# A quarter of the query weights as four loads of one row for each DMA engine, ahead of all other loads

## The chip, the core and the metric

The kernel runs on one core of a Trainium2 chip. The core has a matrix engine (PE), three engines for elementwise work (DVE, ACT, POOL), an engine that issues most transfers (SP), and 16 DMA engines that bring data from HBM into the on-chip memory of 128 partitions (SBUF). The time is the device time of one launch in microseconds (us), the median of several runs.

## The reference, cut to what matters

One token is decoded. It passes through attention over a cache of 65,536 positions (4 key/value heads, 32 query heads of 128) and, beside it, through a gated MLP; a sigmoid gate mixes the two results.

```python
q = (x @ wq).reshape(B, Sq, 32, 128)                    # x: 1 x 1024, wq: 1024 x 4096
scores = einsum('bhqd,bhkd->bhqk', q, k) * 128 ** -0.5  # k, v: 4 heads x 65536 x 128
a = einsum('bhqk,bhkd->bhqd', softmax(scores), v) @ wo  # wo: 4096 x 1024
z = gelu(x @ w_in)                                      # w_in: 1024 x 3584
b = (z[:1792] * (w_sp * layernorm(z[1792:]) + b_sp)) @ w_out
g = sigmoid((x * gate_w).sum())
out = g * a + (1 - g) * b
```

All of it is bf16. Everything that is read is 162 MB, of which the caches are 134 MB and the query weights `wq` 8.4 MB.

## The kernel before

**Loads.** All large loads stand in one list, `stream`, in a fixed order: the query weights, the first two pieces of K, W_in, two more pieces of K, W_out, and then K and V pieces in turn, and Wo in six loads at the end. Their target is a ring in SBUF, five slots of 16,384 bf16 elements a partition (32 KB): slots 0 to 2 mostly for K (`KR = 3`), from `VB = KR * SUB` on for V and the weights. `load` (L308) puts an entry into the list. `issue` (L377) issues entries in order, all on SP (L390), until one is reached whose place in the ring still holds something that hasn't been used; `done` (L399) marks a piece as used and calls `issue` again. What a load has to wait for is found by the recorder (`Recorder`, L18): every operation names what it reads and writes, and `plan` derives the semaphore waits. Each engine runs its own list in program order.

`rows(A_wq, 0, 8)` (L316) lays the 1024 rows of the query weights on 128 partitions, eight neighbouring rows each: partition p holds rows 8p to 8p+7, a run of 64 KB. The load is split over the 16 DMA engines, eight partitions each.

`emit` moves the first `R.ahead = 2` issues of SP (the query weights and the first K load) and the first four of ACT (x, the gate's weights and two scalars, L289) ahead of the barrier at the start of the program, so they are issued before the other engines begin.

**Around the query.** POOL and DVE first build constants (an identity `idb`, masks, selectors; L271 to L425). DVE spreads x over eight rows (`xm`, L428), PE turns it with eight small matmuls into the columns of `xT` (L433), so that column c holds x[8p + c] on partition p, and DVE copies it (L437). L438 to L452 bring the scalars and the gate into place. Then PE multiplies the eight columns with the query weights: for each column c four column groups times two halves, 64 matmuls of 512 columns into `ob`, four of which run side by side; it waits for `xT` and for the whole load of the weights:

```python
wqs, keys = use(("wq", 0))
def f(e):
    for c in range(KC):                      # KC = 8
        for cg in range(4):
            for s in range(2):
                ...                          # L261 / L263
P("PE", f, r=["xT"] + keys, w=["ob"])
done(("wq", 0))
```

After it the place of the weights is free and SP issues W_in. The query is copied, transposed and spread (L468 to L483) and POOL puts it into `qpad` (`q_piece`, L489), which is set to zero at the start (L275).

**The rest.** K pieces are transposed by DVE (L503) and multiplied with the query by PE (`k_piece`), followed by maximum, exponential (ACT, L535), transposition of the probabilities (L540) and the product with V (`pv_piece`). The MLP is done between the first K pieces. At the end PE multiplies with Wo (`wo_rows`, `wo_piece`, L713), the last quarter of which comes in three loads (`WO_CUT`), DVE copies the result (L776), and SP stores it (L367).

Of the kernel before, what the change touches and what calls it, by code (L numbers as in the profile page):

```python
# [138 lines left out]
def bass_gated_mix__gqa_block_cached__mixer_gmlp__decode_kernel(  # L139
# [22 lines left out]
    KC = D // 128  # L162
# [6 lines left out]
    SUB = 16384  # L169
# [15 lines left out]
    OFF = {}  # L185
    cur = 0

    def region(name, nbf):
        nonlocal cur
        OFF[name] = cur  # L190
        cur += (nbf + 15) // 16 * 16

    for name, n in [
        ("M16", 32), ("MQ", 32),
        ("RING", NSUB * SUB), ("KT", NKT * 4096), ("SC", NSC * 2048), ("PSB", 2 * 1024), ("PTSB", 2 * 1024),
        ("QPAD", 4 * QP), ("IDB", 128), ("BM", 256), ("SEL", 16 * 32),
        ("XT", KC), ("WB", 2), ("WBB", 4), ("ONEB", 128),
        ("MAXC", 2 * total), ("LP", 2 * total), ("COLS", 2 * 64), ("DM", 64), ("ONES", 256), ("QALL", 128), ("OVZ", 32 * OC + 31), ("E4Z", 128), ("MHALF", 4),
        ("YB", FC), ("OROW", QW),
    ]:  # L200
        region(name, n)
    NA = (cur + 63) // 64 * 64
    arena = nc.alloc_sbuf_tensor("arena", [128, NA], BF16)

    def ab(name, n, o=0):
        return arena[:, OFF[name] + o:OFF[name] + o + n]

    def af(name, n, o=0):
        return arena[:, OFF[name] + 2 * o:OFF[name] + 2 * (o + n)].bitcast(F32)

    def vw(base, off, dims, p0=0, np_=128):
        ps = base.ap[0][0]
        return bass.AP(tensor=base.tensor, offset=base.offset + off + p0 * ps,
                       ap=[[ps, np_]] + [list(d) for d in dims])

    idb, bm, ones = ab("IDB", 128), af("BM", 128), af("ONES", 128)
    sel, m16, mq = ab("SEL", 512), af("M16", 16), af("MQ", 16)
    xT, wb, wbb, oneb = ab("XT", KC), ab("WB", 2), af("WBB", 2), ab("ONEB", 128)
    qpad, qall = ab("QPAD", 4 * QP), ab("QALL", 128)
    maxc, lp, colt = af("MAXC", total), af("LP", total), af("COLS", 64)  # L220
    mhalf = af("MHALF", 2)
# [27 lines left out]
    ob, mb, fb = obt[:, :], mbt[:, :], fbt[:, :]  # L249
    tb = scp[:, 1024:1536]  # L250
    tbh = tb.bitcast(BF16)
    KSC = lambda n: ("scp", n % 2)
    KTB = ("scp", 1)

    R = Recorder()
    P = R.op

    def mm(e, loaded, *a, **kw):

        if not loaded:  # L260
            return e.matmul(*a, **kw)  # L261
        with nc.discard():
            one = e.matmul(*a, **kw).ins  # L263
        return e.add_instruction(dataclasses.replace(one, name=nc.get_next_instruction_name(), ldweights=False))
# [21 lines left out]
    def small(dst, src, key):  # L286
        def f(e):
            with nc.allow_non_contiguous_dma(reason="a few bytes"):
                return e.dma_start(dst, src)  # L289
        P("ACT", f, w=[key], dma="l" + key)  # L290
# [3 lines left out]
    xm = ab("SC", 1024, 3 * 2048 + 512)  # L294
# [8 lines left out]
    stream = []  # L303
    place = {}

    GRAN = 1024

    def load(keys, src, off):  # L308

        n = len(stream)  # L310
        w = src.shape[1]
        for i, key in enumerate(keys):
            place[key] = (n, off + i * (w // len(keys)), w // len(keys))
        stream.append((keys, off, src))

    def rows(w, i, c):  # L316

        return w[128 * c * i:128 * c * (i + 1), :].rearrange("(p c) n -> p (c n)", c=c)
# [9 lines left out]
    WQ_N = HQ * Dh  # L328
    VB = KR * SUB

    def load_k(n, slot):
        load([("k", n)], kv(A_k_cache, n), slot * SUB)

    def load_k2(n, slot):
        load([("k", n), ("k", n + 1)], kv(A_k_cache, n, True), slot * SUB)

    def load_v2(n, off):
        load([("v", n), ("v", n + 1)], kv(A_v_cache, n, True), off)

    load([("wq", 0)], rows(A_wq, 0, 8), VB)  # L340
    load_k2(0, 0)
    load([("win", 0)], rows(B_w_in, 0, 8), VB)
    load_k(2, 2)
# [2 lines left out]
    for i in range(6):  # L346
        a = 2 * i + 4
# [18 lines left out]
    def store():  # L366
        P("SP", lambda e: e.dma_start(out[0, 0].rearrange("(q n) -> q n", n=QW), osrc), r=["orow"],  # L367
          w=["out"], dma="out")

    issued = [0]  # L370
    used = set()
    owner = {}

    def grains(off, w):
        return list(range(off // GRAN, (off + w + GRAN - 1) // GRAN))

    def issue():  # L377

        while issued[0] < len(stream):
            n = issued[0]  # L380
            keys, off, src = stream[n]
            w = src.shape[1]
            gr = grains(off, w)
            if any(k not in used for x in gr if x in owner for k in owner[x]):
                return
            for j, x in enumerate(gr):
                owner[x] = (keys[j * len(keys) // len(gr)],)
            if n == len(stream) - 1:
                store()
            P("SP", lambda e, o=OFF["RING"] + off, w=w, src=src: e.dma_start(arena[:, o:o + w], src),  # L390
              w=[("slot", x) for x in gr], dma="s%d" % gr[0])
            issued[0] += 1

    def use(key):
        n, off, w = place[key]
        assert n < issued[0], key
        return arena[:, OFF["RING"] + off:OFF["RING"] + off + w], [("slot", x) for x in grains(off, w)]

    def done(key):  # L399
        used.add(key)  # L400
        issue()

    issue()


# [8 lines left out]
      r=["m32"], w=["sel"])  # L414
    P("DVE", lambda e: e.tensor_reduce(mq, vw(idf, 0, [[1, 16], [16, 8]]), AXX, ALU.add), r=["idf"], w=["mq"])
    P("DVE", lambda e: e.tensor_reduce(mhalf, vw(idf, 0, [[32, 2], [64, 2], [1, 32]]), mybir.AxisListType.XY, ALU.add),
      r=["idf"], w=["mhalf"])
# [3 lines left out]
    KSE = "sele"  # L421
    for fe in range(4):
        P("POOL", lambda e, fe=fe: e.tensor_copy(vw(sele, 128 * fe, [[32, 4], [1, 32]]),
                                                vw(idb, 64 * (fe // 2) + fe % 2, [[0, 4], [2, 32]])),
          r=["idb"], w=[KSE])  # L425


    P("DVE", lambda e: e.tensor_tensor(vw(xm, 0, [[128, 8], [1, 128]], 0, 8), vw(xrow, 0, [[0, 8], [1, 128]], 0, 8),  # L428
                                       vw(idb, 0, [[1, 8], [0, 128]], 0, 8), ALU.mult), r=[KX, "idb"], w=["xm"])

    def f(e):
        for c in range(KC):
            ins = e.matmul(tb[:, c:c + 1], vw(xm, c, [[8, 128]], 0, 8), oneb[0:8, 0:1], start=(c == 0),  # L433
                           stop=(c == KC - 1), skip_group_check=True)
        return ins
    P("PE", f, r=["xm", "oneb"], w=[KTB])
    P("DVE", lambda e: e.tensor_copy(xT, tb[:, 0:KC]), w=["xT", KTB])  # L437
    P("PE", lambda e: e.matmul(mb[:, 0:2], oneb[0:1, :], wb[0:1, :], start=True, stop=True),  # L438
      r=["oneb", "wsp", "bsp"], w=["mb"])
    P("DVE", lambda e: e.tensor_copy(wbb, mb[:, 0:2]), w=["wbb", "mb"])  # L440
# [5 lines left out]
      r=["ones", "gs"], w=[KTB])  # L446
# [4 lines left out]
      r=["g"], w=["omg"])  # L451
    P("DVE", lambda e: e.tensor_scalar(mhalf, mhalf, col(C_G), None, op0=ALU.mult), r=["mhalf", "g"], w=["mhalf"])  # L452


    wqs, keys = use(("wq", 0))

    def f(e):
        for c in range(KC):
            for cg in range(4):
                for s in range(2):  # L460
                    o = WQ_N * c + 512 * (4 * s + cg)
                    ins = mm(e, s > 0, ob[32 * cg:32 * cg + 1, 512 * s:512 * (s + 1)], xT[:, c:c + 1], wqs[:, o:o + 512],
                                   start=(c == 0), stop=(c == KC - 1), tile_position=(0, 32 * cg),
                                   skip_group_check=True)
        return ins
    P("PE", f, r=["xT"] + keys, w=["ob"])
    done(("wq", 0))
    P("DVE", lambda e: e.tensor_copy(psb[0:97, :], ob[0:97, :]), w=["psb", "ob"])  # L468
# [20 lines left out]
    def q_piece(g):  # L489
        for pb in range(4):  # L490
            P("POOL", lambda e, pb=pb: e.tensor_copy(vw(qpad, 24 + 32 * pb, [[QP, 4], [1, 8]], 32 * pb, 32),  # L491
                                                    vw(qall, 8 * g, [[32, 4], [1, 8]], 32 * pb, 32)),
              r=["qall"], w=["qpad"])

    nkt = [0]

    def k_piece(n, p):
        if n % NP == 0 and p == 0:
            q_piece(n // NP)
        sl, keys = use(("k", n))  # L500
        i = nkt[0]
        nkt[0] += 1
        P("DVE", lambda e: e.transpose(ktb(i).bitcast(F32), sl[:, 4096 * p:4096 * (p + 1)].bitcast(F32)),  # L503
          r=keys[4 * p:4 * p + 4], w=[("kt", i % NKT)])
        if p == 3:
            done(("k", n))

        def f(e):
            for fe in range(4):
                f2, ev = fe // 2, fe % 2  # L510
                o = QP * fe + 24 - 8 * p
                for b in range(2):
                    ins = mm(e, b > 0, sc_ps(n)[:, 512 * b:512 * (b + 1)], qpad[:, o:o + 128],
                                   vw(ktb(i), 2048 * b + 64 * f2 + ev, [[128, 16], [2, 32]]),
                                   start=(p == 0 and fe == 0), stop=(p == 3 and fe == 3), skip_group_check=True)
            return ins
        P("PE", f, r=["qpad", ("kt", i % NKT)], w=[KSC(n)])
# [258 lines left out]
    P("DVE", lambda e: e.tensor_copy(orow[0:W0 + NW, :], fb[0:W0 + NW, 0:QW]), w=["orow", "fb"])  # L776
    store()

    R.ahead = 2
    R.early = 4  # L780
    R.emit(nc)

# [27 lines left out]
```

## Time and profile before

| | us |
|---|---|
| median of 3 runs | 381.1 (380.82 to 381.35) |
| the profiled execution | 381.14 |
| its span, first to last instruction | 379.8 |
| DMA traffic in it | 162 MB, 427 GB/s over the span |
| PE busy | 231.7 |
| DVE busy | 204.5 |
| first load issued | 0.00 |
| query matmuls | 22.98 to about 29.5 |
| first K piece's transposes begin | 41.24 |
| last matmuls on Wo begin | 376.03 |
| output store issued | 378.59 |

Times in the profile are counted from the first instruction of the span. A line such as "L503" is a line of the kernel's file; L261 and L263 are the two lines of the helper `mm`, which records a matmul with and without a weight load. "SPq" is a transfer issued by SP. The DMA view of a short window cuts the window into 40 equal slices, and shows for each the busy share in tenths and the rate in GB/s; both are counted at the slice in which a packet starts if packets are longer than a slice. The records of single DMA packets (start, duration, size, queue) lie in the same trace: q1 is SP's queue, q10 ACT's, q8 and q14 bring instructions.

### The profile page before, as it was taken

What the parts mean: (1) busy time and instruction counts of PE and PEld (TensorE: products, weight loads), DVE (VectorE), ACT (ScalarE), POOL (GpSimd) and SP (SyncE); (2) the same over time, 40 slices, a digit from 0 to 9 for tenths busy, and PEclk for the clock granted to TensorE, in tenths of its full rate; (3) what the DMA queues carried; (4) which work ended last, traced back from release to release, by engine and by line L of the source; (5) the groups of instructions that cost most, each with busy time, mean ns of one, the idle gap of its engine ahead of it and who ended that gap; (6) DMA issues with size and microseconds to landing.
All of it is one profiled execution on the core that took longest, in us unless ns stands there. A gap on an engine that the chain in (4) does not pass through costs nothing.

```text
span 379.8 us, 2579 instructions
## 1 busy us (share of the span) xinstructions
PE 231.7 (61%) x1447; PEld 57.6 (15%) x836; DVE 204.5 (54%) x162; ACT 23.3 (6%) x24; POOL 9.4 (2%) x37
## 2 busy tenths in 40 slices
PE   0061389467558924894787129952895983639376
PEld 0010011011101200121111001220121110212024
DVE  4011496878379524965892248745874872312020
ACT  1000000010420000002100000022000000220010
POOL 6000000000000000000000000000000000000000
PEclk9997599698959975999799758985899896959789
DMA  9998999998999999999998999999999999989996
GB/s 435 435 428 386 469 388 438 435 470 377 437 442 442 435 437 435 435 400 442 478 435 386 428 442 442 443 442 428 428 397 437 473 442 442 430 386 424 431 430 271
DMA packets 4255, 162.17 MB, mean 427 GB/s; under 512 B 533, under 2 KB 533, under 8 KB 789
## 3 DMA queue, kind: packets, MB, share of 16 engines
q1 hardware_dynamic: 4208, 162.01, 99.0%
q8 instruction: 9, 0.15, 0.1%
q10 hardware_dynamic: 36, 0.00, 0.0%
q14 instruction: 2, 0.01, 0.0%
HBM read 162.01 MB, written 0.00 MB: 427 GB/s over the span
## 4 chain that ended last, share of the span: by engine, by line
DMA 64%; DVE 18%; PE 17%; issue 1%; ACTq 0%; SPq 0%; DVEq 0%
DMA arena<-in_A_k_cache_dram 41%; DVE arena L503 15%; DMA arena<-in_A_v_cache_dram 10%; DMA arena<-in_A_wo_dram 8%; DMA arena<-in_B_b_sp_dram 5%; PE scp L261 5%; PE scp L263 5%; PE obt L261 4%; PE obt L263 3%; DVE arena L540 1%; PE fbt L713 1%; ACTq L289 0%; DVE arena L574 0%; DVE arena L576 0%; SPq L390 0%
## 5 line engine op out<-in xcount | busy, mean ns | idle before, releaser
L503 DVE STREAM_TRANSPOSE arena<-arena 128x2048 f32<-128x2048 f32 x64 | 142.9, 2283 | 45.2 <-DMA arena<-in_A_k_cache_dram 31.1
L261 PE MATMUL scp<-arena 128*128 128x512 bf16 (+1 forms) x273 | 110.5, 421 | 85.4 <-DVE arena L503 84.9
L263 PE MATMUL scp<-arena 128*128 128x512 bf16 (+1 forms) x279 | 110.9, 416 | 0.3 <-issue 0.3
L261 PE MATMUL obt<-arena 128*64 128x512 bf16 (+2 forms) x334 | 62.7, 420 | 21.3 <-DMA arena<-in_A_v_cache_dram 21.3
L263 PE MATMUL obt<-arena 128*64 128x512 bf16 (+2 forms) x334 | 62.1, 416 | 0.0
L261 PEld LDWEIGHTS scp<-arena 128*128 128x128 bf16 (+1 forms) x275 | 27.4, 103 | 195.8 <-issue 97.7
L540 DVE STREAM_TRANSPOSE arena<-arena 128x2048 bf16<-128x2048 bf16 x7 | 16.2, 2311 | 29.5 <-PE obt L263 27.3
L261 PEld LDWEIGHTS obt<-arena 128*64 128x64 bf16 (+1 forms) x334 | 18.2, 113 | 74.4 <-issue 56.7
L535 ACT ACTIVATE arena<-arena 128x2048 bf16<-128x2048 f32 x8 | 16.0, 2002 | 218.1 <-DVE arena L532 195.0
L520 DVE TENSOR_SCALAR_CACHE_REDUCE arena<-scp 128x2048 f32<-128x2048 f32 x8 | 18.3, 2292 | 16.0 <-PE scp L263 16.0
L581 PE MATMUL mbt<-arena 128*128 128x128 bf16 x16 | 2.0, 267 | 12.6 <-DVE arena L576 12.6
L543 DVE STREAM_TRANSPOSE arena<-arena 128x1024 bf16<-128x1024 bf16 x2 | 2.5, 1247 | 12.5 <-PE obt L263 12.5
L491 POOL COPY arena<-arena 32x32 bf16<-32x32 bf16 x16 | 3.3, 204 | 233.5 <-PE scp L263 209.3
L569 DVE RECIPROCAL arena<-mbt 128x1 f32<-128x1 f32 x4 | 0.6, 139 | 15.8 <-PE mbt L564 15.8
L532 DVE TENSOR_REDUCE arena<-mbt 128x1 f32<-128x32 f32 x4 | 0.8, 192 | 14.0 <-PE mbt L529 14.0
L438 PE MATMUL mbt<-arena 1*128 1x2 bf16 x1 | 0.2, 158 | 12.6 <-DMA arena<-in_B_b_sp_dram 12.6
L440 DVE COPY arena<-mbt 128x2 f32<-128x2 f32 x1 | 0.2, 160 | 12.6 <-PE mbt L438 12.6
L433 PE MATMUL scp<-arena 8*128 8x1 bf16 x8 | 0.7, 199 | 8.3 <-DVE arena L428 8.3
L776 DVE CAST arena<-fbt 36x128 bf16<-36x128 f32 x1 | 0.3, 283 | 10.0 <-PE fbt L713 10.0
L713 PE MATMUL fbt<-arena 128*32 128x128 bf16 x128 | 4.1, 220 | 1.3 <-DMA arena<-in_A_wo_dram 1.3
L468 DVE CAST arena<-obt 97x1024 bf16<-97x1024 f32 x1 | 1.2, 1224 | 5.6 <-PE obt L263 5.6
L713 PEld LDWEIGHTS fbt<-arena 128*32 128x32 bf16 x128 | 3.6, 97 | 2.9 <-DMA arena<-in_A_wo_dram 1.9
(91 smaller groups left out, 54.9 us busy)
## 6 DMA issues: line engine op xcount, KB each, us to landing
arena<-in_A_k_cache_dram SPq DMA_DIRECT2D x6, 4096.0 KB, 33.1
arena<-in_A_v_cache_dram SPq DMA_DIRECT2D x2, 4096.0 KB, 26.8
arena<-in_B_w_in_dram SPq DMA_DIRECT2D x1, 7168.0 KB, 29.6
arena<-in_A_wo_dram SPq DMA_DIRECT2D x3, 2048.0 KB, 34.2
arena<-in_B_w_out_dram SPq DMA_DIRECT2D x1, 3584.0 KB, 20.6
arena<-in_A_wo_dram SPq DMA_DIRECT2D x1, 1280.0 KB, 30.9
arena<-in_A_wo_dram SPq DMA_DIRECT2D x1, 512.0 KB, 31.7
arena<-in_A_wo_dram SPq DMA_DIRECT2D x1, 256.0 KB, 31.4
```

Of the source, the lines that this page charges most:

```text
L261: return e.matmul(*a, **kw)
L263: one = e.matmul(*a, **kw).ins
L468: P("DVE", lambda e: e.tensor_copy(psb[0:97, :], ob[0:97, :]), w=["psb", "ob"])
L491: P("POOL", lambda e, pb=pb: e.tensor_copy(vw(qpad, 24 + 32 * pb, [[QP, 4], [1, 8]], 32 * pb, 32), vw(qall, 8 * g, [[32, 4], [1, 8]], 32 * ...
L503: P("DVE", lambda e: e.transpose(ktb(i).bitcast(F32), sl[:, 4096 * p:4096 * (p + 1)].bitcast(F32)), r=keys[4 * p:4 * p + 4], w=[("kt", i % ...
L520: P("DVE", lambda e: e.tensor_scalar(scs(j), scp[:, :], 0.0, None, op0=ALU.add, op1=ALU.max, accum_out=maxc[:, j:j + 1]), w=[("sc", j % 2) ...
L532: P("DVE", lambda e: e.tensor_reduce(gcol(g, K_NB), mb[:, 0:32], AXX, ALU.min), w=[("nb", g), "mb"])
L535: P("ACT", lambda e: e.activation(psb2, scs(j), ACTF.Exp, bias=gcol(j // 2, K_NB), scale=SCALE, accum_out=lp[:, j:j + 1]), r=[("sc", j % 2 ...
L540: P("DVE", lambda e: e.transpose(ptsb2, psb2), r=["psb"], w=[("ptsb", 0), ("ptsb", 1)])
L543: P("DVE", lambda e: e.transpose(ptsb(n), ab("PSB", 1024, 1024 * (n % 2))), r=["psb"], w=[("ptsb", n % 2)])
L581: ins = e.matmul(mb[:, 0:128], sel[:, 128 * c:128 * (c + 1)], osc[:, 128 * c:128 * (c + 1)], start=(c == 0), stop=(c == 3))
L713: ins = e.matmul(fb[32 * b:32 * (b + 1), 0:QW], ovz[:, z:z + 32], sl[:, o:o + QW], start=False, stop=(i == 3 and c == 7), tile_position=(0 ...
```

## The change

The query weights are split by rows. Rows 0 to 767 go as before, now six neighbouring rows (48 KB) on each of the 128 partitions. Rows 768 to 1023 come first, in four loads of 16 rows of the target: load r writes partitions 32 + r, 36 + r, ... 92 + r, each with four neighbouring rows (32 KB). They land in slot 2 of the ring, on partitions 32 to 95. The partitions 0 to 31 and 96 to 127 of that place are set to zero by DVE and POOL (`zp0`, `zp1`), so that the matmul can run over all partitions. `xT2` has ten columns more than `xT`, six for the large part and four for the small one; for the latter x runs past its end, into a stretch that POOL sets to zero (`xmz`), or meets the zeros of the weights. The matmuls run over ten columns of weights instead of eight and wait for all of the loads and for both memsets; W_in and the next K load wait for these matmuls. SP issues six loads ahead of the barrier instead of two.

```diff
-    xT, wb, wbb, oneb = ab("XT", KC), ab("WB", 2), af("WBB", 2), ab("ONEB", 128)
+    xT2, xT = ab("XT", 18), ab("XT", KC)
+    wb, wbb, oneb = ab("WB", 2), af("WBB", 2), ab("ONEB", 128)
...
+    NA4 = 4
+    KB6 = KC - 2
+    def load_a(r):
+        src = vw(A_wq, (128 * KB6 + NA4 * r) * WQ_N, [[1, NA4 * WQ_N]], 0, 1)
+        src = bass.AP(tensor=src.tensor, offset=src.offset, ap=[[4 * NA4 * WQ_N, 16], [1, NA4 * WQ_N]])
+        stream.append(((("wqa", 0),), 2 * SUB, src, r))
...
-    load([("wq", 0)], rows(A_wq, 0, 8), VB)
+    for r in range(4):
+        load_a(r)
+    load([("wq", 0)], rows(A_wq, 0, KB6), VB)
...
+            if r is not None:
+                for x in grains(off, w):
+                    owner[x] = keys
+                a = arena[:, OFF["RING"] + off:OFF["RING"] + off + w]
+                dst = bass.AP(tensor=a.tensor, offset=a.offset + (32 + r) * a.ap[0][0],
+                              ap=[[4 * a.ap[0][0], 16], [1, w]])
+                P("SP", lambda e, dst=dst, src=src: e.dma_start(dst, src), w=[("wqa", r)], dma="wqa%d" % r)
+                issued[0] += 1
+                continue
...
+    P("POOL", lambda e: e.memset(ab("SC", 128, 3 * 2048 + 512 + 1024), 0.0), w=["xmz"])
...
-        for c in range(KC):
-            ins = e.matmul(tb[:, c:c + 1], vw(xm, c, [[8, 128]], 0, 8), oneb[0:8, 0:1], start=(c == 0),
-                           stop=(c == KC - 1), skip_group_check=True)
+        at = [(c, 8) for c in range(KC)] + [(c, KB6) for c in range(KB6)] + [(128 * KB6 - 32 * NA4 + c, NA4) for c in range(NA4)]
+        for c, (o, st) in enumerate(at):
+            ins = e.matmul(tb[:, c:c + 1], vw(xm, o, [[st, 128]], 0, 8), oneb[0:8, 0:1], start=(c == 0),
+                           stop=(c == len(at) - 1), skip_group_check=True)
         return ins
-    P("PE", f, r=["xm", "oneb"], w=[KTB])
-    P("DVE", lambda e: e.tensor_copy(xT, tb[:, 0:KC]), w=["xT", KTB])
+    P("PE", f, r=["xm", "xmz", "oneb"], w=[KTB])
+    P("DVE", lambda e: e.tensor_copy(xT2, tb[:, 0:KC + KB6 + NA4]), w=["xT", KTB])
+    zp = [af("RING", SUB // 2, SUB)[32 * i:32 * (i + 1), :] for i in (0, 3)]
+    P("DVE", lambda e: e.memset(zp[0], 0.0), w=["zp0"])
+    P("POOL", lambda e: e.memset(zp[1], 0.0), r=[KSE, "xmz"], w=["zp1"])
...
+    wqa = ab("RING", NA4 * WQ_N, 2 * SUB)
+    keys = keys + [("wqa", r) for r in range(4)] + ["zp0", "zp1"] + [("slot", x) for x in grains(2 * SUB, SUB)]
+    used.add(("wqa", 0))
...
-        for c in range(KC):
+        parts = [(wqa, c) for c in range(NA4)] + [(wqs, c) for c in range(KB6)]
+        for i, (w, c) in enumerate(parts):
+            z = KC + (KB6 + c if w is wqa else c)
...
-              r=["qall"], w=["qpad"])
+              r=["qall", "zp1"], w=["qpad"])
...
-    R.ahead = 2
+    R.ahead = 6
```

More of the change, by code (lines that the diff above doesn't have):

```diff
@@ L196, in bass_gated_mix__gqa_block_cached__mixer_gmlp__decode_kernel @@
         ("QPAD", 4 * QP), ("IDB", 128), ("BM", 256), ("SEL", 16 * 32),
-        ("XT", KC), ("WB", 2), ("WBB", 4), ("ONEB", 128),
+        ("XT", 18), ("WB", 2), ("WBB", 4), ("ONEB", 128),
         ("MAXC", 2 * total), ("LP", 2 * total), ("COLS", 2 * 64), ("DM", 64), ("ONES", 256), ("QALL", 128), ("OVZ", 32 * OC + 31), ("E4Z", 128), ("MHALF", 4),
@@ L313, in load @@
             place[key] = (n, off + i * (w // len(keys)), w // len(keys))
-        stream.append((keys, off, src))
+        stream.append((keys, off, src, None))
     def rows(w, i, c):
@@ L380, in issue @@
             n = issued[0]
-            keys, off, src = stream[n]
+            keys, off, src, r = stream[n]
             w = src.shape[1]
+            if r is not None:
[7 more added lines that the diff above has]
+                continue
             gr = grains(off, w)
@@ L461, in f @@
                     o = WQ_N * c + 512 * (4 * s + cg)
-                    ins = mm(e, s > 0, ob[32 * cg:32 * cg + 1, 512 * s:512 * (s + 1)], xT[:, c:c + 1], wqs[:, o:o + 512],
-                                   start=(c == 0), stop=(c == KC - 1), tile_position=(0, 32 * cg),
+                    ins = mm(e, s > 0, ob[32 * cg:32 * cg + 1, 512 * s:512 * (s + 1)], xT2[:, z:z + 1], w[:, o:o + 512],
+                                   start=(i == 0), stop=(i == len(parts) - 1), tile_position=(0, 32 * cg),
                                    skip_group_check=True)
```

## The prediction

> **What bounds the kernel now.** I read the page first, for which engine carries the span, then the chain of waits, then the DMA view in short windows at both ends of the run, then the timeline around the query projection.
>
> ```profile
> q1 hardware_dynamic: 4208, 162.01, 99.0%
> q8 instruction: 9, 0.15, 0.1%
> ...
> DMA 64%; DVE 18%; PE 17%; issue 1%; ACTq 0%; SPq 0%; DVEq 0%
> ```
>
> The first line says that the packets of SP's queue fill 99.0% of what 16 DMA engines could do in 379.8 us. Sixteen 64 KB packets of 2.418 us each (the median of the packet records) make 434 GB/s, and every packet's median added up and divided by 16 is 374.2 us. The last line is the chain of waits: mostly landings, with DVE and PE work behind them. No DMA engine idles between 2 and 375 us. So the time is: when the engines begin, plus 374.2 us, plus what delays an engine, plus the tail behind the last landing. The changed loads are the very first ones, so I looked at 0 to 3 us, in 40 slices of 0.075 us, where GB/s counts a packet in the slice in which it starts (one 64 KB packet is 874):
>
> ```profile
> DMA  0000000000000999900900009090000000000000
> GB/s 0 0 1 0 0 0 0 0 0 0 0 0 0 5243 1748 1748 1748 0 0 1748 0 0 0 0 874 0 874 0 0 0 0 0 0 0 0 0 0 0 0 0
> ```
>
> SP issues the first load at 0.00. Six engines start at 1.00 us, six more by 1.27, then two at 1.45, one at 1.81, one at 1.96: a stagger of 0.96. By the records the first packets end at 4.07 to 4.67. Less the normal 2.418, the engines have in effect begun at 1.65 to 2.25, so most first packets hold about 0.65 us of extra (3.07 against 2.42; the last starter only 0.05). The lag isn't worked off; 18 to 24 us, in slices of 0.15 us:
>
> ```profile
> GB/s 0 0 0 437 3932 1311 437 874 0 0 0 0 0 0 0 0 0 0 0 0 3495 2185 437 874 0 0 0 0 0 0 0 0 0 0 0 0 3495 2185 437 874
> ```
>
> Three rounds of packets, each 2.42 us after the last, each with a pack and three stragglers. The middle round, at 21.0, is the first of the K load: the boundary between two loads costs nothing visible. The other end, 375 to 378 us (0.075 us a slice), and the output store, 378.5 to 379.5 (0.025 us):
>
> ```profile
> DMA  9975969899984819284837455544242900000000
> ```
>
> ```profile
> GB/s 0 0 0 0 0 0 0 0 0 0 0 0 0 0 0 0 0 0 0 0 0 0 0 0 0 0 0 0 0 0 0 0 0 0 20 31 21 10 0 0
> ```
>
> From 376 on only about nine engines still work, until 377.43. The page counts nine instruction packets (q8, 16 KB each); the records put eight of them before the end, each 0.88 to 0.97 us long and with one data packet of about 0.5 us extra behind it. So a hit costs one engine some 1.4 us, and the hit engines are those that end last; among them the ends are about 0.45 us apart. The last line is the store of one small packet for each of eight engines: issued at 378.59, its packets start at 379.37 to 379.44, that is 0.78 us after the issue and within 0.07 us. What follows the last landing:
>
> ```profile
> 376.03 2.16 PE fbt L713 x64
> 378.28 0.28 DVE arena L776
> ```
>
> Wo's last three pieces feed those 64 matmuls, which had waited for DMA at 373.05 (1.07 us) and 376.03 (0.26); an earlier landing passes on to the end one for one, up to about 1 us.
>
> **The change part by part.** *The first load.* It removes one load of 128 rows of 64 KB (eight packets an engine) and puts in four of 16 rows of 32 KB (one packet an engine) and one of 128 rows of 48 KB. Bytes stay. Start of the first packets: the nearest row for one packet an engine is the store, 0.78 us and a stagger of 0.07, against 1.00 and 0.96 now; an upper end is that nothing moves. I take the store's row, since its shape is that of the new load. Of the 0.65 extra I keep all (bounds: 0.05, as the last starter shows, and 0.76, the longest). In effect the engines then begin at 0.78 + 0.65 = 1.43 to 1.50. The engine that began first gains 0.22 us, the last one 0.75. Which of them ends last isn't in the records; the 0.45 us spread among the late enders looks like the start's, so I count a gain of 0.22 + 0.33 = 0.55.
>
> *Its price.* Four more load boundaries: the one at 21.0 us lies within the 2.42 rhythm to some 0.02 us, so 4 x 0.02 = 0.08. Four 32 KB packets take 4 x 1.213 = 4.85 and eight of 48 KB some 14.52 (from 28 KB: 1.062 and 56 KB: 2.116), together 0.03 over eight of 2.418. Sum 0.1 us. From above: no boundary in this trace has its next load issued only 0.4 us before it, so one could cost the first packet's 0.65 each time; that is the slow rival.
>
> [...]
>
> *The query projection.* It grows from 16 groups of four matmuls (0.43 us each until 28.9 us) to 20: +1.7 us at most; ten more transposing matmuls are +0.8 (eight took 0.66). Two new memsets of 8192 f32 a partition: L282's 1024 in 0.91 us makes 7.3 us on DVE, L277's 1055 in 0.98 makes 7.6 on POOL, from about 10 us on; DVE's delays L440 to about 18 us, POOL's the wait of q_piece. Side by side both end by 18, one after the other by 25; the weights land at 22. Small POOL memset: 0.2 us ahead of the x transposes. What covers this:
>
> ```profile
> 22.98 0.60 PE L261 MATMUL obt<-arena 128*1 128x512 bf16 x4
> 29.56 0.33 SPq L390 DMA_DIRECT2D arena<-in_B_w_in_dram  x1
> 32.38 0.94 POOL L491 COPY arena<-arena 32x32 bf16<-32x32 bf16 x4 [23.71 <-DVE arena L483]
> 41.24 4.50 DVE L503 STREAM_TRANSPOSE arena<-arena 128x2048 f32<-128x2048 f32 x2 [8.92 <-DMA arena<-in_A_k_cache_dram]
> ```
>
> The query has to be there by 41.24 and SP's W_in issue by 40.35, when its first packet follows K's. In the worst order the projection ends at 25 + 6.5 + 1.7 = 33.2 and the query stands at 37: nothing on the path, 7 us left for the issue. Queued behind SP's wait (now also for the matmuls on the new rows) are W_in and the next K load, both behind the same wait already. The b_sp chain (L438, 21.53) comes earlier, as its eight turns behind 64 KB packets become four behind 32 and four behind 48 KB.
>
> *SP's six issues ahead.* 0.37 to 0.42 us each, 2.3 us in all against 0.85. The other engines start at 2.25, half a microsecond after ACT's last issue; now perhaps 2.8. All of that set-up waits for weights at 22 us.
>
> *PE's code.* About 44 more PE instructions on 2283 (some 254 for each instruction packet) move the hits some 7 us forward and add none before the end. A second hit on one engine would cost 1.4.
>
> Sum: 381.14 for the profiled execution (379.83 and 1.31 around it; the median is 0.04 lower), -0.55 + 0.10 = -0.45, so 380.65 from the median; I say 380.6.
>
> **The rivals.** *Fuller gain:* the late enders are late starters (0.75), and the smaller first packets hold less extra (0.65 down to 0.3): 1.1 - 0.1 = 1.0, 380.1. For it: the last starter's packet had hardly any extra. Against: the fifteen others had 0.44 to 0.76. *Nothing:* what comes before 1.65 us is the memory's waking, not the load's shape, and the engines that end last began early: 0.1 less at most, 381.0. For it: packets started from 1.00 to 1.27 all end at 4.07 to 4.29. *Bubbles (slower):* with one packet an engine, each load runs dry before the next one's packet is there, and the 0.65 is paid four more times: 381.1 - 0.55 + 2.6 = 383.2. It decides once a following load's packets arrive over 1.21 us after the previous ones. Against: SP's issues are 0.43 apart. *Late query:* W_in's issue passes 40.35; it takes 11 us of new delay where I find 4 at most. With a second instruction hit (382.0) it shares a small chance.
>
> **How the numbers follow.** Forecast 0.37, fuller gain 0.36, nothing 0.14, bubbles 0.09, late query or second hit 0.04. About 0.2%, 0.76 us, is what a measurement of this kernel can tell from no change: under 380.34 is faster, over 381.86 slower. The forecast's own spread (0.2 to 0.85 gained) puts 0.08 of its 0.37 below 380.34. Faster: 0.36 + 0.08 = 0.44; same: 0.29 + 0.14 = 0.43; slower: 0.09 + 0.04 = 0.13. The range goes from the fuller gain with its extra all gone (381.1 - 0.78 - 0.60 + 0.1 = 379.8) to 381.5, "nothing" with boundaries at 0.1 each; bubbles stay outside.
>
> **What would show it.** Right: in the first 3 us sixteen packets start within 0.2 us of each other, before 1.0; later rounds show no stragglers; the last data packet ends near 376.9; W_in is issued between 28 and 34 us. Wrong: slices without packets between 1.5 and 7 us (bubbles), first starts still at 1.0 with stragglers (nothing), DMA idle near 40 us (late query), or a last engine with two q8 packets.

## The result: slower, 382.33 us against 380.92

The changed kernel takes 382.33 us (382.13 to 382.55), the one before 380.92 in the same comparison: a ratio of 1.0036, with a 95% interval of 1.0026 to 1.0046, or 1.41 us more. The profiled execution of the changed kernel has a span of 380.9 us.

The page of the changed kernel: the traffic is the same, the share of the queue lower, and the chain of waits again mostly landings.

```profile
q1 hardware_dynamic: 4336, 162.01, 98.7%
q8 instruction: 9, 0.15, 0.1%
...
DMA 57%; DVE 20%; PE 20%; ACT 1%; SPq 1%; issue 1%; DVEq 0%
```

The DMA view from 0 to 3 us in slices of 0.075 us (a 32 KB packet is 437, the small figures are ACT's tiny loads), and SP's timeline, with the first line of the one before for comparison:

```profile
DMA  0000000000000000009999900900909000000000
GB/s 0 0 0 0 0 0 0 0 0 0 0 0 0 0 17 10 0 0 1748 874 1748 874 437 0 0 437 0 0 437 0 437 0 0 0 0 0 0 0 0 0
```

```profile
0.00 2.51 SPq L401 DMA_DIRECT2D arena<-in_A_wq_dram  x4
2.55 0.59 SPq L411 DMA_DIRECT2D arena<-in_A_wq_dram  x1
3.19 0.44 SPq L411 DMA_DIRECT2D arena<-in_A_k_cache_dram  x1
```

Before:

```profile
0.00 0.37 SPq L390 DMA_DIRECT2D arena<-in_A_wq_dram  x1
```

The first packet starts at 1.36 us, not earlier than before (1.00) but later, and the last engine starts at 2.26: the stagger is still 0.90. Each small load holds SP for 0.57 to 0.64 us, and the 48 KB load behind them for 0.59, where the one large load took 0.37. From 0 to 8 us, in slices of 0.2 us (a 32 KB packet is 164, a 48 KB packet 246):

```profile
DMA  0000009995330007993004995900999993339999
GB/s 0 0 0 0 0 10 655 1147 328 164 164 164 0 0 0 330 1481 657 164 0 0 164 819 983 164 492 0 0 328 328 492 328 655 164 164 164 737 1229 983 492
```

The second round starts around 3.2 us, the third around 4.5. The fourth should follow 1.21 us later, around 5.7, and be as narrow as the second; it is smeared from 5.7 to 7.0. By the packet records, the packets of the third round last up to 2.31 us instead of 1.21, those of the engines that escaped there are lengthened in the fourth, and some of the first 48 KB packets by 0.1 to 0.3. After 8 us the rounds are regular again, but an engine's delay stays with it; 18 to 24 us, 0.15 us a slice, the rounds now in two clusters:

```profile
GB/s 0 0 983 983 1638 983 328 328 0 0 0 0 0 0 655 1311 1311 1311 328 328 0 0 0 0 0 0 0 2185 2185 1748 437 437 0 0 0 0 0 0 0 0
```

At the other end, 376 to 379 us (0.075 us a slice), the last data packet ends at 378.41, 0.98 later than before, and one engine works alone for its last 0.2 us. What follows is as long as it was:

```profile
DMA  7969695946374656462545443219000000000000
```

```profile
377.04 2.16 PE fbt L744 x64
...
379.29 0.28 DVE arena L807
```

To put one number on the start, take for each engine the time less the normal durations of the packets that it has moved so far (the last one in part), and the mean over the 16 engines: the **lag**. At 20 us it is 1.84 us before the change and 2.94 after it, 1.10 more. It consists of the mean start of the first packets (1.24 and 1.61), the mean lengthening of packets (0.60, all in the first ones, and 1.16) and, after the change, 0.1 to 0.2 of idle gaps. As the end waits for the latest engine, a second number helps: the last of the sixteen first packets of W_in starts at 40.93 before and 42.11 after, 1.18 later. These come from one execution of each kernel, the times are medians; the two profiled executions themselves took 381.14 and 382.29, 1.15 apart.

### The profile page after: what moved, and what is told of

It is laid out like the page before. It is cut to its first block, busy times and chain, and to the rows that moved or that the text cites. A ratio compares the mean times of both kernels' runs of the same rounds, so it can differ in the third digit from the quotient of the medians.

```text
span 380.9 us, 2632 instructions
## 1 busy us (share of the span) xinstructions
PE 235.4 (62%) x1473; PEld 58.6 (15%) x854; DVE 211.1 (55%) x163; ACT 23.3 (6%) x24; POOL 16.4 (4%) x39
## 4 chain that ended last, share of the span: by engine, by line
DMA 57%; DVE 20%; PE 20%; ACT 1%; SPq 1%; issue 1%; DVEq 0%
DMA arena<-in_A_k_cache_dram 34%; DVE arena L534 17%; DMA arena<-in_A_v_cache_dram 9%; DMA arena<-in_A_wo_dram 8%; PE scp L262 6%; PE scp L264 5%; DMA arena<-in_A_wq_dram 5%; PE obt L262 4%; PE obt L264 4%; DVE arena L571 2%; SPq L401 1%; PE fbt L744 1%; ACT arena L566 1%; PE fbt L692 0%; ACT arena L688 0%
## 5 line engine op out<-in xcount | busy, mean ns | idle before, releaser
L262 PE MATMUL obt<-arena 128*64 128x512 bf16 (+2 forms) x342 | 64.3, 420 | 21.8 <-DMA arena<-in_A_v_cache_dram 20.3
L264 PE MATMUL obt<-arena 128*64 128x512 bf16 (+2 forms) x342 | 63.6, 415 | 0.0
L462 DVE MEMSET arena<- 32x8192 f32 x1 | 6.9, 6885 | 1.6 <-issue 1.6
L463 POOL MEMSET arena<- 32x8192 f32 x1 | 6.9, 6920 | 0.1
```

Source lines behind the costliest of these rows:

```text
L462: P("DVE", lambda e: e.memset(zp[0], 0.0), w=["zp0"])
L463: P("POOL", lambda e: e.memset(zp[1], 0.0), r=[KSE, "xmz"], w=["zp1"])
```

## The experiments

All times are medians, all differences are against the kernel before in the same comparison. "Small" is a load of fewer than 128 rows. Start, lengthening, lag and W_in are each read from one execution, so small differences in them say little; where start and lengthening do not add up to the lag, the rest is idle gaps.

| kernel, loads in order | mean start | lengthening | lag at 20 us | latest W_in | time | difference | 95% interval of the ratio |
|---|---|---|---|---|---|---|---|
| before: 128 x 64 KB | 1.24 | 0.60 | 1.84 | 40.93 | 380.92 | | |
| changed: 4 of 16 x 32, 128 x 48 | 1.61 | 1.16 | 2.94 | 42.11 | 382.33 | +1.41 | 1.0026 to 1.0046 |
| e1: 64 x 32, 128 x 48 | 1.64 | 0.50 | 2.13 | 41.04 | 381.33 | +0.41 | 0.9999 to 1.0016 |
| e9: 2 of 64 x 16, 128 x 48 | 1.57 | 0.60 | 2.16 | 41.23 | 381.36 | +0.35 | 1.0000 to 1.0018 |
| e10: 4 of 64 x 8, 128 x 48 | 1.53 | 1.00 | 2.60 | 42.05 | 382.14 | +1.13 | 1.0020 to 1.0043 |
| e6: 8 of 16 x 16, 128 x 48 | 1.57 | 1.78 | 4.00 | 43.35 | 383.19 | +2.25 | 1.0045 to 1.0069 |
| e2: 128 x 48, 4 of 16 x 32 | 1.35 | 0.83 | 2.20 | 42.01 | 381.57 | +0.65 | 1.0010 to 1.0028 |
| e17: 128 x 48, 64 x 32 | 1.17 | 0.96 | 2.13 | 41.79 | 381.53 | +0.62 | 1.0009 to 1.0026 |
| e18: 128 x 48, 128 x 16 | 1.26 | 0.80 | 2.05 | 41.45 | 381.61 | +0.56 | 1.0005 to 1.0023 |
| e7: 2 of 128 x 32 | 1.22 | 0.62 | 1.82 | 41.00 | 381.02 | +0.08 | 0.9993 to 1.0010 |
| e14: 4 of 128 x 16 | 1.22 | 0.77 | 2.08 | 41.22 | 381.23 | +0.21 | 0.9997 to 1.0014 |
| e15: 8 of 128 x 8 | 1.62 | 0.22 | 1.80 | 41.03 | 381.06 | +0.04 | 0.9992 to 1.0010 |
| e16: before, with the new work beside | 1.22 | 0.66 | 1.88 | 40.79 | 380.93 | +0.02 | 0.9992 to 1.0010 |

**e1, one small load.** The same rows in the same places, as one load.

```diff
-    for r in range(4):
-        load_a(r)
+    load_a(0)                       # ap=[[NA4 * WQ_N, 64], [1, NA4 * WQ_N]] onto partitions 32 to 95
...
-    R.ahead = 6
+    R.ahead = 3
```

> One load of 64 rows on the partitions 32 to 95 takes the place of the four loads of 16; rows, places, memsets and matmuls stay as in the changed kernel. Theory 1 (the loss comes from four small loads issued one after the other into empty queues): first packets at 1.0 to 1.3 us, no lengthened packets after the first ones, 381.0 to 381.3. Theory 2 (the loss comes from the new memsets and matmuls): 382.3. Theory 3 (rows on half of the partitions, or rows of 48 KB, are slow to load): 382 or more, with long packets in every round of the first load.

381.33, just above theory 1's range and far below the other two. No packet after the first round is lengthened by more than 0.07 us, so places and rows are not slow. But the first packet is still late, at 1.41, and SP's issue took 0.60. Its first 3 us:

```profile
GB/s 0 0 0 0 0 0 0 0 0 0 0 0 0 0 24 3 0 0 437 2621 874 874 0 437 437 0 0 0 1311 0 0 0 0 0 0 0 0 0 0 0
```

**e2, the large load first.**

```diff
+    load([("wq", 0)], rows(A_wq, 0, KB6), VB)
     for r in range(4):
         load_a(r)
-    load([("wq", 0)], rows(A_wq, 0, KB6), VB)
```

> The load of 48 KB rows is issued first, then the four loads of 16 rows, then K; all else as in the changed kernel. Theory 1 (small loads cost only while the queues are empty): first packets at 1.0 as before the change, the four small loads at 4 x 1.21 us without extra, 381.0 to 381.2. Theory 2 (memsets, matmuls): 382.3. Theory 3 (the small loads are slow in themselves): their packets are over 1.3 us long here too, 381.8 or more.

381.57. The first packet is at 1.01 and SP's first issue takes 0.37, and the small loads' own packets, now at 16 to 22 us, are not lengthened: theory 3 falls. The time fits none of the three: 0.65 us are lost, in first packets of 48 KB that last up to 1.8 us longer than normal. That was not expected; e17, e13 and e18 take it up.

**e3 and e4, what else happens at that time.** e3 issues only the four small loads ahead of the barrier, e4 takes ACT's tiny loads out.

```diff
e3:  R.ahead = 6  ->  R.ahead = 4
e4:  R.early = 4  ->  R.early = 0
```

> Only the four small loads are issued ahead of the barrier, the 48 KB load and K behind it. Packets lengthened by 0.3 to 1.1 us stand between 4.4 and 7.5 us in the changed kernel. If the descriptors of the two large loads cause them, they come about 1.5 us later here, and the time stays at 382.3. If the other engines' start behind the barrier (4.0 us in the changed kernel) causes them, they come about 0.8 us earlier. If the large loads' packets arrive too late, slices without packets appear near 6 to 7 us, and it is 383 or more.

> ACT issues its four tiny loads behind the barrier, no longer beside SP's first issues. If ACT's issues are what lengthens SP's from 0.37 to 0.58 to 0.64 us and moves the first packet from 1.00 to 1.36, these go back to 0.4 and 1.0, and the time is 381.7 to 382.0. If it is the form of the loads (every fourth partition), they stay, and so does 382.3.

e3: 382.19 (+1.27, 1.0022 to 1.0046). e4: 382.34 (+1.42, 1.0023 to 1.0048). Neither moves the loss. In e3 the large loads were issued only 0.6 and 0.4 us later (3.16 and 3.55), not 1.5 as I had thought, and the long packets again start mostly in the third and fourth rounds, between 4.3 and 6.1 us (one stands at 3.4); so e3 rules out the other engines' start as the cause, which came 0.88 earlier (3.15 instead of 4.03), but not the large loads. In e4 SP's issues still take 0.57 to 0.59 and the first packet stays at 1.40: ACT's loads are not it.

**e5, two loads of 32 rows on every second partition.**

```diff
-            ap=[[4 * NA4 * WQ_N, 16], ...]      # source;  target every fourth partition
+            ap=[[2 * NA4 * WQ_N, 32], ...]      # source;  target every second partition, r = 0, 1
```

> Two loads of 32 rows (two 32 KB packets an engine) take the place of the four of 16. Lag is the time less what the bytes moved so far take at normal packet durations, the mean over the 16 engines at 20 us: 1.84 us before the change, 2.94 with four loads, 2.13 with one. Theory 1a (each small load more costs its share while the queues are empty): lag about 2.4, time 381.7. Theory 1b (only from the third load on are packets lengthened, as seen): lag about 2.1 to 2.2, 381.3 to 381.4. If loads of half of the partitions start late whatever their number, the first packets stay at 1.36 to 1.45.

385.38 (+4.44, 1.0102 to 1.0173), and no answer to its question: after the first ones the packets of the two loads lasted about 2.37 us instead of 1.21, which alone is 4.6 us for four packets an engine. The profiled execution is not a typical one: it took 390.33, the other five 385.34 to 385.43. Which engine writes which row of such a load isn't in the records.

**e6, eight small loads.**

```diff
-    for r in range(4): load_a(r)       # 16 rows of 32 KB
+    for r in range(8): load_a(r)       # 16 rows of 16 KB: half r % 2 of the rows of load r // 2
...
-    R.ahead = 6
+    R.ahead = 10
```

> Eight loads of 16 rows of 16 KB (0.61 us a packet) take the place of the four of 32 KB; SP issues ten loads ahead of the barrier. If SP's rate of issue (0.58 to 0.64 us for such a load) is what the engines wait for, they now stand still or have lengthened packets between nearly all loads: lag 4.0 to 5.5, time 383.4 to 385. If the cost is one of bytes or of places (partitions 32 to 95), lag and time stay near 2.9 and 382.3.

383.19, lag 4.00, of which 0.65 is idle gaps between packets: bytes and places are the same in sum, so small loads in front are paid by their number, or by how little each holds (256 KB here, 512 KB in the changed kernel). Its first 8 us show the smearing of all rounds from the second on:

```profile
GB/s 0 0 0 0 0 10 246 737 82 246 85 85 988 82 82 328 328 410 82 246 164 164 246 328 492 328 246 328 246 246 574 246 164 492 246 164 328 410 164 410
```

**e7, e14, e15: two, four and eight loads of 128 rows,** with no other part of the change but eight more transposing matmuls.

```diff
-    load([("wq", 0)], rows(A_wq, 0, 8), VB)
+    for i in range(n):                          # n = 2, 4, 8
+        load([("wq", i)], rows(A_wq, i, 8 // n), VB + 8 // n * i * WQ_N)
...
-    R.ahead = 2
+    R.ahead = n + 1
```

> The kernel before, with the query weights as two loads of 128 rows of 32 KB (four rows each) instead of one of 64 KB; no memsets, no matmuls more. If the late first packet (1.36 to 1.41 instead of 1.00) belongs to loads on fewer than 128 partitions, it is at 1.00 here, the lag 1.85 to 1.95 and the time 380.9 to 381.1. If it belongs to rows of 32 KB or to any split of the first load, it is at 1.3 to 1.4, with 381.2 to 381.5.

> The kernel before with the query weights as four loads of 128 rows of 16 KB, issued one after the other ahead of the barrier. If any three or more loads issued in the first microseconds lengthen packets: lag 2.3 to 2.9, 381.5 to 382.3. If only loads of fewer than 128 rows do: lag 1.85, 381.0, as with two loads of 128 rows.

> The same with eight loads of 128 rows of 8 KB, nine issues ahead of the barrier. By count: lag near 4 (as with eight loads of 16 rows), 383. By form: lag 1.9 to 2.0 (64 packets of 8 KB an engine, a few ns more each), 381.0 to 381.3.

381.02, 381.23 and 381.06; two and eight are the kernel before within 0.1 us; four lose 0.21 with an interval that reaches down to no difference, and a lag of 2.08 between the two that were expected. The lag with eight is 1.80, against 4.00 with eight small ones. So it is not the number of loads alone, nor rows shorter than 64 KB, nor issues in quick succession. First packets are at 0.99 to 1.05 in all three. For the late start this separates rows from bytes: e1 and e14 begin with 2 MB, e9 and e15 with 1 MB, and those of 64 rows are late, those of 128 are not. For the lengthened packets it does not: the kernels that pay for several loads in front (the changed one, e6, e10) have 256 or 512 KB in each load, and the kernels that do not pay (e7, e9, e14, e15) have 1 MB or more. Loads of 128 rows with 512 KB in each were not tried.

**e8, the kernel before without ACT's loads in front.**

```diff
-    R.early = 4
+    R.early = 0
```

> The kernel before with ACT's four tiny loads behind the barrier. If these, issued beside SP's first, are what spreads the first packets over 0.96 us, all sixteen start within 0.3 us, the lag falls to about 1.6 and the time to 380.6 or 380.7, under both kernels. If not, the lag stays at 1.8 to 1.9 and the time at 380.9.

381.00 (0.9992 to 1.0010), lag 1.90. The stagger isn't ACT's either.

**e9, e10: two and four loads of 64 rows.**

```diff
-    for r in range(4): load_a(r)       # 16 rows of 32 KB
+    for r in range(n): load_a(r)       # n = 2: 64 rows of 16 KB;  n = 4: 64 rows of 8 KB
```

> Two loads of 64 rows of 16 KB on the partitions 32 to 95 take the place of the four of 16 rows of 32 KB. (The earlier two loads on every second partition were at half the rate, 2.36 us for 32 KB, so they could not tell what a second load costs.) Lag was 2.13 us with one load, 2.94 with four, 4.00 with eight, some 0.27 for each more. If the number of loads into empty queues is what costs: lag 2.4, time 381.5 to 381.7. If only loads with one row for each engine cost: lag 2.1 to 2.2, 381.3.

> Four loads of 64 rows of 8 KB on the partitions 32 to 95. If the number of loads counts: lag 2.9, lengthened packets between 4 and 8 us, time 382.2 to 382.4, as with four loads of 16 rows. If the form with one row for each engine counts: lag 2.1 to 2.3, 381.3 to 381.5.

Two: 381.36, no more than one, so my 0.27 for each load was wrong between one and two. Four: 382.14, with packets lengthened from 4.6 us on and in ten of the sixteen first 48 KB packets. So one row for each engine is not the point; four loads of 64 rows cost nearly what four of 16 cost (both are 512 KB a load, and 1 MB in the run with two). The window from 4 to 8 us with two loads (slices of 0.1 us), for comparison with the smeared one above, has its rounds of 0.6 us and then the 48 KB packets close together:

```profile
GB/s 492 164 328 330 499 661 661 164 164 492 328 819 655 164 0 655 328 819 655 164 0 655 328 655 655 164 164 983 983 1966 1475 983 492 983 492 0 0 0 0 0
```

**e11, the large load third.** Two small loads, the 48 KB load, the other two.

```diff
-    for r in range(4):
+    for r in range(2):
         load_a(r)
     load([("wq", 0)], rows(A_wq, 0, KB6), VB)
+    for r in range(2, 4):
+        load_a(r)
```

> The changed kernel with the 48 KB load issued third, after two small loads and before the other two. If small loads cost only until a large load has filled the queues: lag 2.3 to 2.5 and no lengthened packets where the last two small loads run, time 381.4 to 381.7. If the third load's packets are lengthened whatever it is, or the small loads cost in any place: lag 2.8 or more, 382.1 or more.

382.24 (+1.23, 1.0020 to 1.0045), lag 2.53, latest W_in 42.14. Lag said the one and time the other; I go by the time. The packets lengthened are now, but for one, 48 KB packets that start between 4.9 and 6.8 us, two by 0.7 and 0.8, the rest by 0.1 to 0.3: the time in the run is nearly the same, the load that is hit another. So it isn't only the small loads' own packets that are slow.

**e12, 64 rows from partition 0 on** (a single execution).

> One look at the first packets only: one load of 64 rows of 32 KB as in the run with one load, but on the partitions 0 to 63. If a load is late because it has fewer than 128 rows, SP's issue takes 0.57 to 0.60 us and the first packet starts at 1.36 to 1.45. If it is late because it does not begin at partition 0, they are 0.37 and 1.00. [...]

SP's issue takes 0.55 us, the first packet is at 1.35: late for having fewer than 128 rows, not for where it begins. And the time was 400.7, where the kernel before took 381.01. Its packets last 2.57 us instead of 1.21, and so do, to a lesser degree, those of the loads behind it:

```profile
12.00:50.00 38.00, 8.34 (x95) 2.36 (x55) 9.62 (x11) 0.17 (x1) 4.44 (x5) 0.90 0.98 341
50.00:100.00 50.00, 30.76 (x162) 6.25 (x82) 33.12 (x25) 1.51 (x2) 0.00 (x0) 0.77 0.99 372
100.00:370.00 270.00, 179.70 (x961) 41.64 (x507) 161.56 (x111) 19.26 (x19) 2.44 (x12) 0.82 1.00 434
```

The last column is the rate in GB/s: 341 and 372 until 100 us, then 434. As e5's profiled execution took 5 us more than its others, this one may not be typical either.

**e13, the small loads behind the barrier.** e2, with one load issued ahead.

```diff
-    R.ahead = 6
+    R.ahead = 1
```

> The 48 KB load alone is issued ahead of the barrier; the four small loads and K follow behind it, when the queues hold 15 us of work. Rows, places, memsets and matmuls stay. If the small loads cost only by being issued within the first 3 us, while the queues are being filled: first packets at 1.0, lag 1.85 to 1.95, the latest engine's first W_in packet at about 41.0 (40.93 before the change, 42.11 in the changed kernel), time 381.0 to 381.2. If they cost wherever they stand: lag over 2.2, 381.6 or more.

381.67 (+0.65, 1.0010 to 1.0028), with a lag of only about 2.0 and a latest W_in at 42.39: the time fits the second, the lag neither. Issued at 2.13 to 3.98 us, behind the large load, the small ones leave the kernel where e2 has it.

**e16, the work beside the loads alone.** The kernel before with `xmz`, `zp0`, `zp1`, ten more transposing matmuls, and two more groups of weights in the query matmuls that meet an x of zeros.

> The kernel before with its one load of 128 rows of 64 KB, and of the change only the work beside the loads: both long memsets, the small one, ten more transposing matmuls, and ten groups of weights instead of eight (two of them with an x of zeros). If that work is off the path: lag 1.8 to 1.9, 381.0 to 381.1. If it costs what one load of 64 rows did (381.3 to 381.4), its share of the loss is 0.35 and the late first packets cost nothing.

380.93, lag 1.88: nothing.

**e17, e18: the 48 KB load in front, and behind it one load of 64 rows, or one of 128.**

```diff
e17 (from e1):       load([("wq", 0)], rows(A_wq, 0, KB6), VB); load_a(0)
e18 (from before):   load([("wq", 0)], rows(A_wq, 0, 6), VB)
                     load([("wq", 1)], A_wq[768:1024, :].rearrange("(p c) n -> p (c n)", c=2), VB + 6 * WQ_N)
```

> The 48 KB load first and then one load of 64 rows on the partitions 32 to 95, all else as in the changed kernel. If the 0.35 to 0.41 us that one or two such loads in front cost are their late first packets (1.38 to 1.41 instead of 1.00): first packets at 1.00 here, lag 1.85 to 1.95, 381.0 to 381.1. If the split or the memsets and matmuls cost it: 381.3 or more.

> The kernel before with the query weights as a load of 128 rows of 48 KB and, right behind it, one of 128 rows of 16 KB: the same cut of the weights as with the 48 KB load in front and one 64-row load behind it, but no load of fewer than 128 rows, and nothing of the work beside the loads. In that run the first packets of 48 KB were lengthened by 0.96 us on average (0.60 before the change), lag 2.13, 381.53. If the 64-row load behind them did that: extra 0.60 to 0.70, lag 1.8 to 1.9, 380.9 to 381.1 here. If rows of 48 KB do it: extra 0.8 or more, lag over 2.0, 381.3 or more.

381.53 and 381.61. e17's first packets are at 1.01, on time, and it loses 0.62 all the same, so it does not price the late start. e18 has no small load and no memsets, and loses 0.56 us: what it shares with e2, e13 and e17, which lose 0.62 to 0.65, is the load of 48 KB rows in front. Its packets are lengthened by 0.80 us on average and up to 1.73 (0.60 and 0.76 before the change); e14's are by 0.77 on average, for a loss of 0.21, so the mean lengthening alone doesn't settle it. Its start, 0 to 3 us:

```profile
GB/s 0 0 0 0 0 0 0 0 0 0 0 0 0 3277 1311 2621 655 0 0 0 0 655 655 655 0 0 0 0 655 0 0 0 0 0 0 0 0 0 0 0
```

Starts are on time and staggered as ever; the loss is inside the packets. Against e18, small loads behind a large load cost 0.1 us by the medians, four of them (e2) or one (e17), which is less than the intervals can tell from nothing.

No variant is faster than the kernel before beyond its interval; none of the runs here points to one.

## Why the prediction was wrong

Against the forecast of 0.45 us less, the kernel takes 1.41 more. Three terms of the sum failed: two gains that did not come (0.22 and 0.33, and the first turned into a loss of about 0.4 by the medians), and a price put at 0.10 that was 0.8 to 1.0.

**The start (predicted 0.22 us earlier for the first engine).** This step failed. I took 0.78 us from issue to first packet from the output store, whose issue itself takes 0.31; the small load's takes 0.58, and its first packet comes 0.78 after the issue's end. Later, not earlier, by 0.36, in every kernel that begins with a small load (1.35 to 1.41) and in none that begins with 128 rows (0.99 to 1.05). e1 and e9, which have the late start and hardly any other lengthening, lose 0.41 and 0.35 us; each interval reaches down to no difference, so the size is not shown.

**The stagger (predicted to vanish, 0.33).** The sixteen first starts still lie 0.90 apart. The store's 0.07 was that of eight packets of 256 bytes, and it didn't carry over. With one row an engine the first and the last engine begin 0.90 us apart, with eight 0.96. The extra that I kept at 0.65 was 0.49 in the mean of the first 32 KB packets.

**The price of four more loads (predicted 0.10).** This is the larger error: four small loads cost 0.8 to 1.0 us more than one or two (e10 against e9: 0.78; the changed kernel against e1: 1.00). I read it off a boundary whose next load had been waiting for 20 us and wrote beside it that no row showed a load issued just before it. The bubble rival named that gap and its sign was right, but it was mis-sized and its form was off: 0.56 us of lengthening on the mean of the engines where it had 2.6, inside the packets and not as idle slices, and below the point from which it was to decide (SP's issues are 0.63 apart, not over 1.21). Nor does one fixed price for each load fit the runs: four small loads in front cost 1.41 us in all, four behind a filled queue 0.1 by the medians (e2 against e18), and eight of 128 rows 0.04.

**The work beside the loads (predicted nothing).** Right, and shown by e16. The profile has the terms as worked out: both memsets side by side, 6.9 us each (7.3 and 7.6 predicted), W_in's issue at 29.39.

```profile
10.52 6.92 POOL L463 MEMSET arena<- 32x8192 f32 x1
...
13.50 6.88 DVE L462 MEMSET arena<- 32x8192 f32 x1 [1.64 <-issue]
...
23.12 0.60 PE L262 MATMUL obt<-arena 128*1 128x512 bf16 x4 [1.57 <-DMA arena<-in_A_wq_dram]
...
29.39 0.33 SPq L411 DMA_DIRECT2D arena<-in_B_w_in_dram  x1
...
42.43 4.50 DVE L534 STREAM_TRANSPOSE arena<-arena 128x2048 f32<-128x2048 f32 x2 [10.35 <-DMA arena<-in_A_k_cache_dram]
```

The first K piece is transposed 1.19 us later, because its bytes are. SP's six issues took 3.63 us instead of 2.3, and the other engines began at 4.03 instead of 2.8; that too is covered. The instruction packets (q8) remained nine, the ninth in the last 0.4 us of the loads (378.06 of 378.41), as before (377.39 of 377.43).

**That a shift at the start passes to the end.** Right in kind: it held for the loss too. Among the profiled executions, each against the 381.14 of the kernel before, the changed kernel is 1.15 us longer with its latest W_in packet 1.18 later; in e10 it is 0.86 with 1.12, in e6 2.33 with 2.42, in e2 0.95 with 1.08. But in e13 it is 0.46 with 1.46, and in e3 1.01 with 2.61. So the latest engine at 40 us doesn't fix the end by itself; nor does the mean lag, which rose by 0.36 in e2.

**What stays open.** Why the issue of a small load holds SP longer (0.57 to 0.64 us in the changed kernel, 0.37 for the one large load before it), and why the first 128-row loads right behind small ones take as long (0.57 in e1, 0.59 in the changed kernel, 0.34 in e3, where the barrier stands between). Why four or eight small loads at the start lengthen the packets that run between 4 and 8 us (mean lengthening 1.16 us in the changed kernel, 1.00 in e10, 1.78 in e6, against 0.50 in e1 and 0.60 in e9), while behind a large load issued first the small loads' own packets keep their length (e2) and a large load issued third is itself lengthened (e11, two packets by 0.7 and 0.8 us); whether their few rows or their few bytes do it was not separated. All the small loads also go to the same slot of the ring through an access pattern of their own, which no run took apart from their form. And why 48 KB rows in front lengthen the first packets, but not behind small loads (e1). The runs show when, not by what.

## What to carry to other kernels

In this kernel, where the packets of SP's queue fill 99% of the run, the split and the order of the first loads cost from 0.04 us (e15) to 2.25 us (e6) of 381 in the runs of the table, up to 0.6%, and this was read in the packets of the first microseconds: their starts and their lengths. Here it was best to let the first loads cover all 128 partitions: splitting one of 64 KB rows evenly into two or eight cost nothing that could be measured (0.08 and 0.04 us), splitting it into 48 and 16 KB rows cost 0.56 us, and loads on fewer partitions began later (1.35 to 1.41 us instead of 0.99 to 1.05) and, four of them at 512 KB each, cost up to a microsecond more than one (1.41 against 0.41). The boundary that cost nothing visible in a filled queue (0.02 us, at 21.0) said nothing about one in a queue that was only filling, where four small loads cost 0.8 to 1.0 us more than one or two, and the row of a tiny store (first packet 0.78 us after the issue) said nothing about the start of a load of 512 KB (1.36).

## What the runs showed of the hardware that I had not expected

- A load on the partitions 0 to 63 ran at half the rate (e12: 2.57 us for 32 KB instead of the 1.21 that the same bytes took on 32 to 95, e1). The loads of 128 rows behind it were slow as well, 3.02 us for 64 KB instead of 2.42 until 54 us, and packets were still 12% over normal until about 104 us (e12, a single execution); in e5's profiled execution they were 12% over (2.71 us) until about 56 us. In e5's other five executions, 5 us shorter, the slow packets of the small loads already account for all that was lost, so they can hardly have had it. No run here explains it.
- Instruction packets of 16 KB, nine before the change and nine after it, last 0.88 to 0.97 us in the kernel before, and behind each of the first eight one data packet is lengthened by 0.47 to 0.55. In the kernel before, nine engines ended at 376.8 to 377.4 and the other seven by 376.1.
- After the query weights were cut into eight loads of 128 rows, mean lengthening fell to 0.22 us but twelve engines began at 1.66 to 2.01 instead of 1.0 to 1.3; the lag stayed at 1.80. In that execution the shorter packets made up for the later starts.
